# Decode attention over a long cache: V in runs of eight keys, p turned in column tiles, mask by matmul, another order at the end, and eight filler matmuls a pair

## The chip, the cores and the metric

One core of one Trainium2 chip. The metric is the device time of one execution in microseconds (us), the median of several. Single executions of one kernel lie within about 1% of each other in the first rounds (322.6 to 325.8 us for the kernel before), so differences of less than 1% are read only from several rounds against the kernel before on the same chip. A run that is more than 1.5% above the fastest of its kernel counts as slow; ratios use the other runs alone, unless said otherwise. A ratio is the mean time of one kernel's fast runs over that of the other's in the same rounds, so it is not quite the ratio of the medians quoted beside it.

TensorE is called PE below, its weight loads PEld, VectorE DVE, ScalarE ACT, GpSimd POOL. SPq is the wait of a queue's DMA issues for a free buffer.

## The reference, cut to what matters

```python
# x: 4 tokens x 448, bf16. k_cache, v_cache: [4, 8 heads, 8192, 256] bf16; the last 2,048 keys count
def _A_ref(x, k_cache, v_cache, wq, wo):          # two query heads share one key head
    q = (x @ wq)...
    k, v = k_cache[:, :, Sk - W:, :], v_cache[:, :, Sk - W:, :]
    p = softmax(einsum(q, k) * Dh ** -0.5)
    return einsum(p, v) @ wo
x = x + _A_ref(layernorm(x), ...);  x = x + ffn(layernorm(x))     # layer 1
x = x + _A_ref(layernorm(x), ...);  x = x + ffn(layernorm(x))     # layer 2, same cache, same weights
```

The work is 64 "pairs" of (token, layer, key head). Each pair reads 1 MB of K and 1 MB of V, of which some is still held from the first layer. In all some 105 MB go through the DMA queue in a little over 300 us.

## The kernel before

The kernel is written as a list of operations with ranks and assumed durations. At build time a small scheduler puts them into one fixed order for each engine; nothing is decided on the chip. For one pair, in the order of its chain (cut):

```python
# two loads of K (512 KB each) into free half buffers, each transposed in place by the DVE
g.dma(pos - KLEAD, 1 << 19, ... half[cell[0]] <- ksrc[:, 2048 * hf:2048 * hf + 2048])
g.op(DVE, 1.18, pos, tr, w=(kk[hf],))
# two loads of V: runs of four keys, 2,048 bytes each
vsrc = A_v_cache[t, kvh, s0:s0 + WIN, :].rearrange("(a q g) d -> q a g d", a=4, q=128)
g.dma(pos + VLAG, 1 << 19, ... half[cell[0]] <- vsrc[:, 2 * hv:2 * hv + 2, :, :], run=2048)

def scores(e):                                     # 32 matmuls of 128 columns, four column groups
    for ce in range(8):
        for hf in range(2):
            for x in range(2):
                e.matmul(Sb[s_][qd:qd + 8, 0:128], lhsT=qe[q_]..., rhs=kt[...])
# DVE: maximum of each row; PE: spread it over the partitions; DVE: maximum per head (two columns),
# then a masked sum that picks each partition's own head:
g.op(DVE, 0.2, pos, lambda e: e.scalar_tensor_tensor(out=nb[0:104, 2:4], in0=negm[s_][0:104, :], scalar=1.0,
     in1=nmask[0:104, :], op0=ALU.mult, op1=ALU.mult, accum_out=nb[0:104, 0:1]), ...)
# ACT: exp with that as bias, into praw
def turn(e):                                       # p to the layout that V asks for: 4 matmuls, 128 weights each
    for c in range(2):
        for h in range(2):
            e.matmul(Yb[p_][:, 64 + 32 * c:96 + 32 * c], lhsT=praw[s_][0:104, c0:c0 + 128], rhs=selt[h]...)
# ACT: copy to pT; PE: 16 matmuls with V (pv) of 256 columns; ACT, DVE, PE: the pair's output
```

On PE every matmul is two instructions, a weight load and the matmul itself (4,776 of each in the profile below).

Of the kernel before, what the change touches and what calls it, by code (L numbers as in the profile page):

```python
# [31 lines left out]
KLEAD = 2.2  # L32
VLAG = 1.3
# [12 lines left out]
MMV = 0.034  # L46
TAIL = {"pe": 0.2, "dve": 0.12, "act": 0.15, "pool": 0.1, "sp": 0.05}
# [232 lines left out]
def build(nc, A_x, A_k_cache, A_v_cache, A_wq, A_wo, B_x, B_w_gate, B_w_up, B_w_down, out):  # L280
# [3 lines left out]
    with ExitStack() as es:  # L284
# [12 lines left out]
        pmax = [tiny[:, 12 + s:13 + s] for s in range(NS)]  # L297
        tsel = sb("tsel", [128, 4, B], BF16)
        selt = [sb(f"selt{h}", [128, 2, 4, 2, 2], BF16) for h in range(2)]
        small = sb("small", [128, 11 + 6 * NS + 4 * NY + B + 4], FP32)  # L300
        rmask = small[:, 11 + 6 * NS + 4 * NY:11 + 6 * NS + 4 * NY + B]
        rvec = small[:, 11 + 6 * NS + 4 * NY + B:11 + 6 * NS + 4 * NY + B + 4]
        nmask = small[:, 9 + 2 * NS + 4 * NY:11 + 2 * NS + 4 * NY]
        nbias = small[:, 11 + 2 * NS + 4 * NY:11 + 6 * NS + 4 * NY]
# [21 lines left out]
        praw = [sb(f"praw{s}", [128, 258], BF16) for s in range(NS)]  # L326
        pT = [sb(f"pT{s}", [128, 2, 2, 4, 2, 2], BF16) for s in range(NY)]
# [48 lines left out]
        ivt = identb[:, :].rearrange("p (h x z n) -> p h x z n", h=2, x=2, n=2)  # L376
        for h in range(2):
            for y in range(2):
                for x in range(2):
                    g.op(DVE, 0.1, R0, lambda e, h=h, y=y, x=x: e.tensor_copy(selt[h][:, x, :, y, :], ivt[:, h, x, 0:4, :]),  # L380
                         r=("identb",), w=(f"selt{h}{y}{x}",))
        idq = identb[:, :].rearrange("p (q z n) -> p q z n", q=4, n=2)
        g.op(DVE, 0.2, R0, lambda e: e.tensor_reduce(
            nmask[:, :], idq[:, :, 0:4, :].rearrange("p q a n -> p n q a"), AX.XY, ALU.add), r=("identb",), w=("nmask",))
        for s_ in range(NS):
            g.op(DVE, 0.2, R0, lambda e, s_=s_: e.memset(Sb[s_][:, :], 0.0), w=(f"s{s_}",), bank=(f"S{s_}",))
            g.op(DVE, 0.2, R0, lambda e, s_=s_: e.memset(praw[s_][:, :], 0.0), w=(f"praw{s_}",))
# [44 lines left out]
        def norm(t, rank, x):  # L432
# [30 lines left out]
            gp(lambda e: e.tensor_tensor(s[:, 8:9], s[:, 5:6], expo[:, 0:1], op=ALU.pow), (k + "h", "expo"), (k + "r2",))  # L463
# [15 lines left out]
        def qproj(ts, rank):  # L479
# [5 lines left out]
            for b, (zb, z, bank) in enumerate(banks):  # L485
# [13 lines left out]
                for c0, c1, rr, kw in ((0, 3, XN, dict(w=(z,))), (3, 4, XE, dict(acc=(z,)))):  # L499
                    g.op(PE, 0.43 * (c1 - c0), rank, lambda e, zb=zb, b=b, c0=c0, c1=c1: q_mm(e, zb, b, c0, c1),  # L500
                         r=rr + tuple(f"wq{c}" for c in ((0, 1, 2) if c0 == 0 else (30, 31))), bank=(bank,), **kw)
# [34 lines left out]
        def ffn_row(ts, rank):  # L536
# [24 lines left out]
            for gi, (z, bank, w) in enumerate((("z", "Z", "wg"), ("z2", "Z2", "wu"))):  # L561
                g.op(PE, 1.28, rank, lambda e, gi=gi: gu(e, gi, 0, 3), r=XN + (w + "a",), w=(z,), bank=(bank,))
                g.op(PE, 0.5, rank, lambda e, gi=gi: gu(e, gi, 3, 4), r=XE + (w + "b0", w + "b1"), acc=(z,), bank=(bank,))
# [25 lines left out]
            g.op(PE, 1.5, rank, down, r=("wb", "wd"), acc=tuple(f"row{t}" for t in ts), bank=("A",))  # L589
# [119 lines left out]
        assert len(seq) == 2 * B * HKV and len(set(seq)) == len(seq)  # L709
        k_held, v_held = {}, {}  # L710
# [3 lines left out]
        def pair(pos, si, side, nside, t, layer, kvh):  # L714
# [3 lines left out]
            else:  # L718
                kc, kk = [[], []], [f"k{pos}_{hf}" for hf in range(2)]
                ksrc = A_k_cache[t, kvh, s0:s0 + WIN, :].rearrange("(p j) d -> p (j d)", p=128)  # L720
                for hf, cell in enumerate(kc):
                    g.dma(pos - KLEAD, 1 << 19, lambda e, cell=cell, hf=hf: e.dma_start(  # L722
# [8 lines left out]
            else:  # L731
                vsrc = A_v_cache[t, kvh, s0:s0 + WIN, :].rearrange("(a q g) d -> q a g d", a=4, q=128)
                vs = [[], []]
                for hv, cell in enumerate(vs):
                    g.dma(pos + VLAG, 1 << 19, lambda e, cell=cell, hv=hv: e.dma_start(  # L735
                        half[cell[0]][:, :].rearrange("p (a g d) -> p a g d", a=2, g=4),
                        vsrc[:, 2 * hv:2 * hv + 2, :, :]), None, w=(f"v{t}_{kvh}_{hv}",), run=2048, cell=cell)
# [3 lines left out]
            def scores(e):  # L741
                last = None
                for ce in range(8):
                    for hf in range(2):
                        kt = half[kc[hf][0]][:, :].rearrange("p (l g c r v) -> p c v g l r", l=2, g=4, c=4, v=2)
                        for x in range(2):
                            qd = 64 * hf + 32 * x
                            last = e.matmul(Sb[s_][qd:qd + 8, 0:128], lhsT=qe[q_][:, ce, :, :].rearrange("p a n -> p (a n)"),  # L748
                                            rhs=kt[:, ce // 2, ce % 2, 2 * x:2 * x + 2, :, :], start=(ce == 0),
# [6 lines left out]
            o = g.op(PE, 0.8, pos - SLEAD, scores, r=tuple(kk) + (f"qe{q_}",), w=(f"s{s_}",), bank=(f"S{s_}",))  # L756
            if not keep_k:
                o.rel = tuple(kc)
            g.op(DVE, 0.21, pos, lambda e: e.tensor_reduce(  # L759
                pmax[s_][0:104, :], Sb[s_][0:104, 0:128], AX.X, ALU.max),  # L760
                r=(f"s{s_}",), w=(f"pmax{s_}",), bank=(f"S{s_}",))
            g.op(PE, 0.1, pos, lambda e: e.matmul(  # L762
                Sb[s_][0:104, 128:160].rearrange("p (q x) -> p q x", q=4), lhsT=pmax[s_][0:104, 0:1].broadcast_to([104, 104]),
                rhs=identb[0:104, :].rearrange("p (q x) -> p q x", q=4)[:, :, 0:8], start=True, stop=True,
                skip_group_check=True), r=(f"pmax{s_}", "identb"), w=(f"m{s_}",), bank=(f"S{s_}",))
            g.op(DVE, 0.16, pos, lambda e: e.tensor_reduce(  # L766
                negm[s_][0:104, :], Sb[s_][0:104, 128:160].rearrange("p (k n) -> p n k", n=2), AX.X, ALU.max, negate=True),
                r=(f"m{s_}",), w=(f"negm{s_}",), bank=(f"S{s_}",))
            nb = nbias[:, 4 * s_:4 * s_ + 4]
            g.op(DVE, 0.2, pos, lambda e: e.scalar_tensor_tensor(  # L770
                out=nb[0:104, 2:4], in0=negm[s_][0:104, :], scalar=1.0, in1=nmask[0:104, :], op0=ALU.mult, op1=ALU.mult,
                accum_out=nb[0:104, 0:1]), r=(f"negm{s_}", "nmask"), w=(f"nb{s_}",))
            g.op(SCA, 0.38, pos, lambda e: e.activation(  # L773
                praw[s_][0:104, 2:258].rearrange("p (g r h l) -> p h g r l", g=2, h=2, l=2)[:, 0, :, :, :],
                Sb[s_][0:104, 0:128].rearrange("p (g l r) -> p g r l", g=2, l=2), ACT.Exp, bias=nb[0:104, 0:1]),
                r=(f"s{s_}", f"nb{s_}"), w=(f"praw{s_}",), bank=(f"S{s_}",))

            def turn(e):
                last = None
                for c in range(2):  # L780
                    for h in range(2):
                        c0 = 128 * c + 2 - 2 * h
                        last = e.matmul(Yb[p_][:, 64 + 32 * c:96 + 32 * c], lhsT=praw[s_][0:104, c0:c0 + 128],  # L783
                                        rhs=selt[h][0:104, :, :, :, :].rearrange("p x a y n -> p (x a y n)"),
                                        start=(c == 0 and h == 0), stop=False, skip_group_check=True)
                return last
            g.op(PE, 0.12, pos, turn,
                 r=(f"praw{s_}",) + tuple(f"selt{h}{y}{x}" for h in range(2) for y in range(2) for x in range(2)),
                 w=(f"yp{p_}",), bank=(f"Y{p_}",))
            g.op(SCA, 0.2, pos, lambda e: e.activation(  # L790
                pT[p_][:, :, :, :, :, :].rearrange("p c x a y n -> p (c x a y n)"), Yb[p_][:, 64:128], ACT.Copy),
# [3 lines left out]
                rhs=pT[p_][:, :, :, :, :, :].rearrange("p c x a y n -> p y (c x a) n")[:, 0, :, :], start=False,  # L795
# [6 lines left out]
            def pv(e, hv):  # L802
                last = None
                for a in range(2):
                    for gg in range(4):
                        last = e.matmul(Yb[p_][32 * gg:32 * gg + 4, 256:512],  # L806
                                        lhsT=pT[p_][:, gg % 2, gg // 2, 2 * hv + a, :, :].rearrange("p y n -> p (y n)"),
# [163 lines left out]
```

## Time and profile before

| | before |
|---|---|
| time, median (3 runs at first) | 324.81 us (323.2 to 325.83) |
| span in the profile | 320.3 us |
| bytes moved | 105.16 MB |
| V halves and K halves loaded | 88 and 88, of 512 KB |

The page's rows of clock and DMA, the stages and the chain in the last token are shown and read in the prediction. Four more lines of the same page matter later: the engines' busy times with their instruction counts, the packets, the queue that the page calls "instruction" (packets, MB, share of the 16 DMA engines' span), and the shares of the chain that ended last.

```profile
PE 222.0 (69%) x4776; PEld 136.6 (43%) x4776; DVE 212.4 (66%) x776; ACT 75.2 (23%) x222; POOL 89.2 (28%) x227
...
DMA packets 42369, 105.16 MB, mean 328 GB/s; under 512 B 3144, under 2 KB 7248, under 8 KB 41936
...
q8 instruction: 37, 0.61, 0.7%
...
DMA 40%; PE 23%; DVE 16%; SPq 15%; issue 3%; ACT 2%; POOL 0%; DVEq 0%
```

The reader is to see four things. The chain runs mostly over transfers (DMA 40%, and SPq 15% for loads that wait for a buffer). PE is busy for 69% and stands in the chain with 23%. "issue", time in which an engine waited for nothing that the profile shows, is 3%. And the instruction queue looks like nothing at all, 37 packets and 0.7%.

### The profile page before, as it was taken

To read this page: it belongs to the slowest core of one execution; us is meant where nothing else is said; L and a number is where in the kernel's file an instruction comes from. 1 tells how busy PE (TensorE), PEld (TensorE's weight loads), DVE (VectorE), ACT (ScalarE), POOL (GpSimd) and SP (SyncE) were. 2 spreads that over 40 slices of the span, in tenths; PEclk is the share of its full clock that TensorE was granted. 3 is DMA by queue.
4 is the path that set the end of the run, shared out by engine and by line. 5 is a ranking of instruction groups with operands and counts; after the bars stand their busy time and mean duration, and the time that the engine had idled before them with its cause. 6 is when DMAs were issued, how large, how long until landed. Compare 5 with 4: busy or idle time off the path is not lost.

```text
span 320.3 us, 11153 instructions
## 1 busy us (share of the span) xinstructions
PE 222.0 (69%) x4776; PEld 136.6 (43%) x4776; DVE 212.4 (66%) x776; ACT 75.2 (23%) x222; POOL 89.2 (28%) x227
## 2 busy tenths in 40 slices
PE   1746455546458768678669878796788788688965
PEld 0334232223124445344247555443455446356544
DVE  7396655564244769977656799877677983844642
ACT  0122111121012233212233233132323232023410
POOL 1712211113002333224214323342244322214420
PEclk9999999999999995658875655576958755555975
DMA  7999999999998999999959999999899999708000
GB/s 280 350 404 393 392 395 398 394 393 337 327 395 304 380 393 400 360 398 383 388 205 366 388 398 382 380 389 396 309 315 377 398 368 398 264 8 323 2 3 2
DMA packets 42369, 105.16 MB, mean 328 GB/s; under 512 B 3144, under 2 KB 7248, under 8 KB 41936
## 3 DMA queue, kind: packets, MB, share of 16 engines
q1 hardware_dynamic: 42320, 104.45, 87.9%
q8 instruction: 37, 0.61, 0.7%
q14 instruction: 12, 0.10, 0.1%
HBM read 104.44 MB, written 0.00 MB: 326 GB/s over the span
## 4 chain that ended last, share of the span: by engine, by line
DMA 40%; PE 23%; DVE 16%; SPq 15%; issue 3%; ACT 2%; POOL 0%; DVEq 0%
DMA half<-in_A_k_cache_dram 22%; DMA half<-in_A_v_cache_dram 13%; DVE half L727 9%; PE S L748 8%; SPq L735 6%; SPq L722 6%; PE Y L806 6%; DMA wg_sb<-in_B_w_gate_dram 5%; SPq L407 3%; DVE oh L820 2%; PE Z L558 2%; PE Z L496 1%; PE Z L612 1%; PE Y L826 1%; PE A L858 1%
## 5 line engine op out<-in xcount | busy, mean ns | idle before, releaser
L727 DVE STREAM_TRANSPOSE half<-half 128x1024 uint32<-128x1024 uint32 x88 | 108.8, 1238 | 19.4 <-DMA half<-in_A_k_cache_dram 19.1
L806 PE MATMUL Y<-half,pT 128*4 128x256 bf16 x1024 | 60.8, 356 | 21.0 <-DMA half<-in_A_v_cache_dram 17.9
L816 POOL TENSOR_TENSOR small<-small 128x2 f32<-128x2 f32 x64 | 44.3, 697 | 73.2 <-DVE small L798 66.0
L748 PE MATMUL S<-half,qe 128*8 128x128 bf16 x2048 | 58.9, 279 | 6.0 <-DVE half L727 2.3
L748 PEld LDWEIGHTS S<-half,qe 128*8 128x8 bf16 x2048 | 45.1, 108 | 12.7 <-DVE half L727 3.9
L752 POOL TENSOR_TENSOR qe<-qc,tiny 128x64 bf16<-128x64 bf16 x64 | 18.7, 293 | 93.9 <-PE S L748 71.0
L818 ACT ACTIVATE oh<-Y 128x256 bf16<-128x256 f32 x64 | 24.5, 384 | 77.4 <-PE Y L806 77.2
L806 PEld LDWEIGHTS Y<-half,pT 128*4 128x4 bf16 x1024 | 22.0, 94 | 34.7 <-DMA half<-in_A_v_cache_dram 21.8
L773 ACT ACTIVATE praw<-S,small 104x128 bf16<-104x128 f32 x64 | 22.9, 366 | 58.9 <-DVE small L770 58.7
L820 DVE SCALAR_TENSOR_TENSOR oh<-oh,small,Y 128x256 bf16<-128x256 bf16 x64 | 30.0, 471 | 9.0 <-ACT oh L818 8.2
L759 DVE TENSOR_REDUCE tiny<-S 104x1 bf16<-104x128 f32 x64 | 18.4, 287 | 23.4 <-PE S L748 23.1
L826 PE MATMUL Y<-tiny,oh 128*128 128x2 bf16 x128 | 12.9, 172 | 18.9 <-DVE oh L820 18.4
L790 ACT ACTIVATE pT<-Y 128x64 bf16<-128x64 f32 x64 | 14.1, 223 | 40.9 <-PE Y L783 38.3
L826 PEld LDWEIGHTS Y<-tiny,oh 128*128 128x128 bf16 x128 | 8.3, 107 | 28.1 <-DVE oh L820 24.8
L858 PE MATMUL A<-wo_sb,oT 128*4 128x448 bf16 x140 | 16.3, 454 | 4.3 <-DVE oT L831 4.1
L783 PE MATMUL Y<-selt,praw 104*128 104x32 bf16 x256 | 17.3, 187 | 1.3 <-ACT praw L773 1.3
L793 PE MATMUL Y<-pT,tiny 128*128 128x32 bf16 x64 | 12.5, 197 | 7.9 <-ACT pT L790 7.7
L783 PEld LDWEIGHTS Y<-selt,praw 104*128 104x128 bf16 x256 | 11.7, 104 | 12.5 <-issue 9.1
L766 DVE TENSOR_REDUCE small<-S 104x2 f32<-104x32 f32 x64 | 11.3, 183 | 6.3 <-PE S L762 6.1
L762 PE MATMUL S<-identb,tiny 104*104 104x32 bf16 x64 | 14.4, 240 | 1.6 <-DVE tiny L759 1.5
L459 POOL TENSOR_SCALAR st<-st 128x1 f32<-128x1 f32 x16 | 4.3, 267 | 38.7 <-DVE st L448 38.6
L442 PE MATMUL Z<-st,small 128*128 128x2 f32 x32 | 9.1, 355 | 8.1 <-DVE st L439 7.4
(120 smaller groups left out, 245.9 us busy)
## 6 DMA issues: line engine op xcount, KB each, us to landing
half<-in_A_k_cache_dram SPq DMA_DIRECT2D x88, 512.0 KB, 7.1
half<-in_A_v_cache_dram SPq DMA_DIRECT2D x88, 512.0 KB, 7.1
wo_sb<-in_A_wo_dram SPq DMA_DIRECT2D x8, 448.0 KB, 12.6
wq_sb<-in_A_wq_dram SPq DMA_DIRECT2D x3, 1024.0 KB, 6.8
wd_sb<-in_B_w_down_dram SPq DMA_DIRECT2D x1, 1568.0 KB, 18.3
wg_sb<-in_B_w_gate_dram SPq DMA_DIRECT2D x1, 1344.0 KB, 15.5
wu_sb<-in_B_w_up_dram SPq DMA_DIRECT2D x1, 1344.0 KB, 15.9
wq_sb<-in_A_wq_dram SPq DMA_DIRECT2D x2, 256.0 KB, 10.2
```

Source lines behind the costliest of these rows:

```text
L722: g.dma(pos - KLEAD, 1 << 19, lambda e, cell=cell, hf=hf: e.dma_start(half[cell[0]][:, :], ksrc[:, 2048 * hf:2048 * hf + 2048]), None, w=( ...
L727: return e.transpose(a, a)
L735: g.dma(pos + VLAG, 1 << 19, lambda e, cell=cell, hv=hv: e.dma_start(half[cell[0]][:, :].rearrange("p (a g d) -> p a g d", a=2, g=4), vsrc ...
L748: last = e.matmul(Sb[s_][qd:qd + 8, 0:128], lhsT=qe[q_][:, ce, :, :].rearrange("p a n -> p (a n)"), rhs=kt[:, ce // 2, ce % 2, 2 * x:2 * x ...
L773: g.op(SCA, 0.38, pos, lambda e: e.activation(praw[s_][0:104, 2:258].rearrange("p (g r h l) -> p h g r l", g=2, h=2, l=2)[:, 0, :, :, :], ...
L783: last = e.matmul(Yb[p_][:, 64 + 32 * c:96 + 32 * c], lhsT=praw[s_][0:104, c0:c0 + 128], rhs=selt[h][0:104, :, :, :, :].rearrange("p x a y ...
L806: last = e.matmul(Yb[p_][32 * gg:32 * gg + 4, 256:512], lhsT=pT[p_][:, gg % 2, gg // 2, 2 * hv + a, :, :].rearrange("p y n -> p (y n)"), r ...
L816: g.op(POOL, 0.25, pos, lambda e: e.tensor_tensor(ri[p_][:, :], rs[p_][:, :], expo[:, 1:3], op=ALU.pow), r=(f"rs{p_}", "expo"), w=(f"ri{p_ ...
L818: g.op(SCA, 0.28, pos, lambda e: e.activation(oh[pos % 2][:, :], Yb[p_][:, 256:512], ACT.Copy), r=(f"y{p_}",), w=(f"oh{pos % 2}",), bank=( ...
L820: g.op(DVE, 0.4, pos, lambda e: e.scalar_tensor_tensor(out=oh[pos % 2][:, :], in0=oh[pos % 2][:, :], scalar=lomask[:, 0:1], in1=Yb[p_][:, ...
L826: last = e.matmul(Yb[p_][:, 2 * dh:2 * dh + 2], lhsT=oh[pos % 2][:, :].rearrange("p (m e) -> p e m", e=2)[:, dh, :], rhs=osel[:, :], start ...
L858: last = e.matmul(Ab[32 * k:32 * k + B, 0:D], lhsT=oT[si % 2][:, k % 2, k // 2, :], rhs=wo_sb[:, 4 * kvh + k, :], start=False, stop=False, ...
```

## The change

The intent: V packets of 4,096 bytes instead of 2,048, so that the queue moves the same bytes sooner. That gives p another layout, so its turn is done in sixteen small column tiles instead of four wide ones. The masked sum leaves the DVE and becomes a second small matmul on PE. K of the last pairs is loaded later (tail order). Eight matmuls whose result nobody reads go in front of the scores of each pair, to keep PE's clock up. And the scheduler's assumed durations are set to measured ones. Cut to its core:

```diff
+KTAIL = 0.4
+FILL = 8
-    g.dma(pos - KLEAD, 1 << 19, ...                                     # K
+    g.dma(pos - KLEAD if pos <= LAST1 else pos + KTAIL, 1 << 19, ...
-    vsrc = A_v_cache[...].rearrange("(a q g) d -> q a g d", a=4, q=128)  # runs of 2,048 bytes
+    vsrc = A_v_cache[...].rearrange("(p j) d -> p (j d)", p=128)         # runs of 4,096 bytes
 def scores(e):
+    for i in range(FILL):
+        qd = 32 * (i % 4)
+        e.matmul(Sb[s_][qd:qd + 8, 160:512], lhsT=identb[:, 0:8],
+                 rhs=identb[:, 0:32].unsqueeze(1).broadcast_to([128, 11, 32]), start=True, stop=True, ...)
+def spread(e):                                  # a matmul more: adds "far" where the head isn't the partition's own
+    e.matmul(Sb[s_][0:104, 128:160], lhsT=identb[0:104, 0:104], rhs=far[0:104, :, :]..., start=True, stop=False)
-g.op(DVE, 0.2, pos, lambda e: e.scalar_tensor_tensor(... accum_out=nb[0:104, 0:1]) ...
 def turn(e):
-    for c in range(2):
-        for h in range(2):
-            e.matmul(Yb[p_][:, 64 + 32 * c:96 + 32 * c], lhsT=praw[s_][0:104, c0:c0 + 128], ...)
+    for gg in range(4):
+        for b in range(4):
+            e.matmul(Yb[p_][32 * b:32 * b + 32, 64 + 16 * gg:80 + 16 * gg],
+                     lhsT=praw[s_][0:104, 32 * gg:32 * gg + 32], rhs=selt[b]...)
-g.op(PE, 1.5, rank, down, ...                   # assumed durations, here and in a dozen more places
+g.op(PE, 0.8, rank, down, ...
```

## The prediction

> **What bounds the kernel now.** I read the page first, then the windows by stage, then the chain of waits, then the timeline of single pairs. A "pair" is one (token, layer, head): 64 in all, each with two K halves and two V halves of 512 KB; layer 1 finds 20 heads of both still held, so 88 halves of K and 88 of V are loaded. First the page: the DMA rows by slice, and the groups that the change touches.

> ```profile
> PEclk9999999999999995658875655576958755555975
> DMA  7999999999998999999959999999899999708000
> GB/s 280 350 404 393 392 395 398 394 393 337 327 395 304 380 393 400 360 398 383 388 205 366 388 398 382 380 389 396 309 315 377 398 368 398 264 8 323 2 3 2
> ...
> L748 PE MATMUL S<-half,qe 128*8 128x128 bf16 x2048 | 58.9, 279 | 6.0 <-DVE half L727 2.3
> ...
> L766 DVE TENSOR_REDUCE small<-S 104x2 f32<-104x32 f32 x64 | 11.3, 183 | 6.3 <-PE S L762 6.1
> ```

> The reader is to see a queue that is full up to the 34th slice (8 us each) and a tail of some 30 us with almost no traffic. So two bounds follow each other: the transfers, then a chain of compute. The windows view, by stage, says the same with numbers:

> ```profile
> 100.00:263.00 163.00, 124.76 (x2903) 78.55 (x2899) 128.15 (x442) 48.36 (x145) 51.44 (x125) 0.70 0.98 365
> 263.00:285.60 22.60, 17.50 (x361) 10.84 (x353) 13.23 (x53) 4.48 (x12) 5.74 (x16) 0.50 0.67 255
> 285.60:306.50 20.90, 18.76 (x482) 12.65 (x478) 10.82 (x63) 6.41 (x23) 9.19 (x21) 0.72 0.36 129
> 306.50:320.30 13.80, 7.64 (x213) 6.57 (x201) 4.21 (x22) 1.37 (x4) 1.68 (x6) 0.54 0.01 2
> ```

> (The columns are PE, weight loads, DVE, ACT, POOL, then granted clock, DMA share, GB/s.) From 100 to 263 us the queue ran at 365 GB/s where a full stretch (40 to 60 us, the same view) has 395: 163 x (1 - 365/395) = 12.4 us were lost there to loads that waited for a free buffer. From 263 us it is the last token's own path: its feed-forward and projection (22.6 us), its eight pairs of layer 1 (20.9 us, PE busy 90%) and the closing feed-forward (13.8 us).

> The chain of waits in the second of these stages shows what the DVE does there:

> ```profile
> 273.21 1.15 DVE half L727
> 274.37 0.05 DVE oT L831
> 274.42 1.14 DVE half L727
> ...
> 275.95 1.16 DVE half L727
> ...
> 277.56 1.15 DVE half L727
> 278.71 0.12 DVE xn L446
> 278.83 0.07 DVE st L448
> 278.90 1.43 PE Z L496 x7
> ```

> Transposes of K that is needed only at the very end stand in front of the normalisation that the last token's q waits for.

> And PE's clock, from the timeline, the 32 score matmuls of a pair at 104.9 us and at 262.1 us:

> ```profile
> 104.86 0.62 PE L748 MATMUL S<-half,qe 128*8 128x128 bf16 x32
> ...
> 262.10 1.02 PE L748 MATMUL S<-half,qe 128*8 128x128 bf16 x32
> ```

> The same work takes 0.62 us at full clock and 1.02 us at half. Before 100 us the clock row shows 1.0, yet 32 score matmuls took 1.07 us there (windows of that line): PE was cold, the profile only had no clock event yet.

> [...] clock stretches are multiples of 3.41 us, at 1.0 or 0.5. [...] I counted for every such window the columns streamed, with four matmuls on the four column groups as one. Of the cold windows from 96 us on, all ten with 3,168 or more were followed by full clock, none with 3,108 or fewer; warm windows stayed warm at 2,756 and more, with one exception (2,952). [...] Trace: scores start in groups of four, and (1.02 - 0.62) x 1000 / 8 = 50 ns per group is just what 128 columns differ by. [...] In this trace's packet records 2,048-byte packets have a median of 84 ns and 4,096-byte ones 159 ns, so two of the small cost 9 ns more.

> **The change, part by part.**

> V in runs of eight keys. V packets double from 2,048 to 4,096 bytes, 22,528 of them become 11,264. By mean durations, 22,528 x 89.3 ns / 16 engines = 125.7 us becomes 11,264 x 169.2 / 16 = 119.1 us: 6.6 us. 76 of 88 V halves are issued before 263 us or so, where the queue is the bound: 5.7 us, and I take 5.0, as it isn't always full.

> p turned in column tiles. Four matmuls with 128 weights become sixteen with 32, on four column groups. The four take 0.29 us (timeline). The nearest thing here is the select of the q projection, sixteen matmuls with 32 weights each: 0.30 us. So no cost. exp writes its 128 columns in a plain order; I take its 366 ns as unchanged.

> Mask by matmul. The DVE loses the masked sum and its accumulator read (152 and 82 ns, overlapped to 0.17 us in the timeline): 64 x 0.17 = 10.9 us of DVE's 212, off a chain every pair goes through. The reduce keeps its 32 inputs, so its 183 ns. A second matmul joins the spread: two of them took 0.33 us, one 0.25, so 0.08 us more. Net -0.09 us on the pair's latency; over the eight last pairs 0.7 us.

> Fillers. Eight of 352 columns on four groups are 704 columns in time: 0.29 us at full clock, 0.59 at half, per pair. They come after the waits of the scores, so they fill no idle time; they lengthen the path from a transposed K to its scores. In return they feed the clock: from 99 to 308 us the mean window has 2,568 columns, 22 of 61 windows warm. With 51 pairs there, 704 x 51 / 61 = 589 more make 3,157, about the threshold; I estimate 65% warm instead of 36%. Cost per pair 0.65 x 0.29 + 0.35 x 0.59 = 0.40 us; gain 0.29 x (0.40 on scores + 0.58 on PV + 0.15 on the output projection) = 0.33 us. In the DMA-bound part this is a wash. In the last eight pairs it is not: they run cold from 285.7 to about 297 us, and dense work with fillers (1,024 + 1,024 + 704 + some 400 to 600 columns a pair) passes the threshold within two windows. I take 1.5 us net.

> Tail order. K of the last 11 pairs ranks behind the V of the pair before, not three pairs ahead. Before, six K halves took the free buffers from 263.6 us on, and their transposes stood on the chain above; with K and V in turn about two of the six come after it: 2 x 1.2 = 2.4 us.

> Stalls. The schedule is fixed at build time from assumed durations, and those of PE and POOL become truer if PE is warm; the DVE, over 90% busy from 120 to 140 us, is relieved. I give this a quarter of the 12.4 us: 3.1 us.

> Sum: 5.0 + 0.7 + 1.5 + 2.4 + 3.1 = 12.7 us off 324.8: about 312.

> **The rivals.** (1) The clock doesn't catch. The fillers then cost 0.59 us on pairs with PE already at 15 to 17 of 20 us busy: 51 x 0.59 = 30 us more PE work, perhaps a third of it visible, 10 us. Against it: the score matmuls, of the same shape and columns of weights, evidently count in the windows above. Time then about 322. (2) The clock catches nearly everywhere after 100 us. Then pairs save up to 1.1 us on PE for 0.29, most stalls go, and only the queue and the tail remain: about 303. For it: the mean lies on the threshold, and a faster kernel makes windows denser. Against it: windows with projections or waits have 1,000 to 2,000 columns. (3) V is hidden anyway: the queue's gain turns into waits for free buffers, since a buffer comes free only when PE is done with it. Then the 5 us shrink to 2, time about 315. The 12.4 us of stalls speak for it, the DMA share of 0.98 in that stage against. (4) The new fixed order falls unluckily, with a stall of its own at a token's change like the 4 us around 165 us (slice 21): 317 or so.

> **Range and chances.** Centre 312, between rivals 2 and 3. The five terms are independent enough, each good to a half, and the order of the schedule adds some 4 us either way: 304 to 320 for 8 in 10. Two per cent faster is below 318.3: 0.84. Within two per cent: 0.13. Slower than 331.3 asks for rival 1 and a bad order: 0.03.

> **What would show each step.** V: 4,096-byte packets alone, some 31,100 packets instead of 42,369, full stretches at 400 to 405 GB/s, DMA's share of 16 engines' span times span down 6 us. Mask: no accumulator read in the pairs, DVE busy down about 11 us. Turn: 1,024 records with a busy time near 17 to 20 us. Clock: half-clock stretches after 100 us down to a third of the time; scores with fillers 0.9 us when warm, 1.6 cold. Tail: alternating K and V issues after 250 us, fewer transposes ahead of the last norm, and the stretch from 263 us to the end 52 us instead of 57. I am wrong if the queue is still stalled by 12 us or more, if the clock stays at half for most of the middle, or if the tail is no shorter.

The time of a column, which the fillers' estimate needs, can be read in the trace of the kernel before: where the matmuls with V (L806, 256 columns) follow each other in groups of four, the groups start 109 ns apart at full clock and 213 ns at half (medians). By that, 128 columns differ by 52 ns, and 704 columns are 0.30 us and 0.59 us.

## The result, and the profile after

The changed kernel took 338.1 us (median of 4, 335.38 to 340.1), the kernel before 324.0 in the same rounds (4 runs). The ratio is 1.0426, with a 95% interval of 1.0316 to 1.0536, all runs fast: it is slower, by some 13.8 us. The prediction was wrong in direction. The result is correct.

The changed kernel's page, the same rows as of before, and the groups that the change touched:

```profile
PE 243.9 (72%) x6120; PEld 154.5 (46%) x6120; DVE 207.6 (61%) x651; ACT 75.8 (22%) x222; POOL 89.4 (26%) x227
...
PEclk9975555555569957759976959696755965599785
DMA  7999999999989996998999959999889877876000
GB/s 277 350 405 401 403 403 403 403 383 322 405 313 329 374 352 231 323 406 311 409 372 382 373 188 334 356 358 378 280 286 372 241 269 247 263 286 266 6 3 2
DMA packets 31115, 105.33 MB, mean 312 GB/s; under 512 B 3144, under 2 KB 7248, under 8 KB 30672
...
q8 instruction: 48, 0.79, 0.9%
...
PE 42%; DMA 18%; DVE 15%; SPq 14%; issue 7%; ACT 2%
PE Y L820 9%; PE S L762 9%; DMA half<-in_A_v_cache_dram 9%; DVE half L736 9%; PE S L753 7%; SPq L731 5%; DMA wd_sb<-in_B_w_down_dram 5%; SPq L415 5%; DMA half<-in_A_k_cache_dram 4%; SPq L744 4%; PE Z L566 2%; PE Z L620 2%; PE A L873 2%; DVE oh L835 2%; PE Z L504 2%
...
L762 PEld LDWEIGHTS S<-half,qe 128*8 128x8 bf16 x2048 | 47.5, 106 | 24.9 <-issue 19.1
L753 PE MATMUL S<-identb 128*8 128x352 bf16 x512 | 41.0, 402 | 18.4 <-DVE half L736 7.1
...
L796 PE MATMUL Y<-selt,praw 104*32 104x16 bf16 x1024 | 18.6, 177 | 2.5 <-issue 2.4
```

Much is as predicted: 31,115 packets, 401 to 405 GB/s where the queue is full, 18.6 us of records for the turn. But from the twelfth slice on the GB/s row is mostly below before's, so the queue is filled less than before, not faster. The chain has moved from transfers (40% to 18%) to PE (23% to 42%), the fillers (L753) alone stand in it with 7%, and "issue" rose from 3% to 7%, from 9.6 to 23.7 us of the span. The score's weight loads (L762) were idle 19.1 us on "issue". In the kernel before, the same group (L748) had:

```profile
L748 PEld LDWEIGHTS S<-half,qe 128*8 128x8 bf16 x2048 | 45.1, 108 | 12.7 <-DVE half L727 3.9
```

By stage, the windows of the changed kernel, cut where the chain's stages lie in it (columns as in the prediction):

```profile
100.00:263.00 163.00, 128.79 (x3432) 82.11 (x3425) 112.49 (x326) 42.55 (x129) 48.08 (x117) 0.76 0.92 335
263.00:298.70 35.70, 27.72 (x705) 18.47 (x704) 21.39 (x71) 8.71 (x25) 8.93 (x22) 0.67 0.77 262
298.70:324.50 25.80, 20.05 (x671) 13.89 (x667) 14.53 (x56) 7.55 (x25) 9.57 (x22) 0.93 0.39 146
324.50:338.00 13.50, 7.54 (x205) 6.52 (x205) 4.35 (x23) 1.17 (x4) 1.66 (x5) 0.58 0.01 3
```

From 100 to 263 us the queue had 335 GB/s instead of 365, although PE's clock was higher (0.76 instead of 0.70). The loss is spread. The casts of q into its layout, one for each token's change to the second layer, mark the stages:

| us | 1st token's second q | 2nd | 3rd | 4th | end of span |
|---|---|---|---|---|---|
| before | 103.0 | 165.1 | 230.1 | 284.8 | 320.3 |
| changed | 100.6 | 166.1 | 238.4 | 298.7 | 338.0 |
| lost in the stage | | 3.4 | 7.3 | 5.6 | 3.8 |

What is "issue"? The list of PE's weight-load waits names it (in all, times, longest, in us). First the changed kernel, then before:

```profile
PEld S L762 <- issue: 19.1, 54, 3.7
PEld Y L820 <- DMA half<-in_A_v_cache_dram: 12.6, 15, 1.4
...
PEld S L777 <- issue: 6.3, 12, 3.0
...
PEld Y L796 <- issue: 4.9, 12, 1.9
```

```profile
PEld Y L783 <- issue: 9.1, 30, 0.4
...
PEld Z L450 <- issue: 3.4, 6, 0.9
...
PEld S L762 <- issue: 2.4, 8, 0.4
```

The totals differ by a factor of two, but the last column tells more: in the kernel before, waits on nothing are short, 0.4 us in the pairs; in the changed one they last up to 3.7 us. One of them, in the changed kernel's timeline of PE:

```profile
126.22 0.47 PE L753 MATMUL S<-identb 128*8 128x352 bf16 x8 [0.21 <-DVE half L736]
126.52 0.22 PE L762 MATMUL S<-half,qe 128*8 128x128 bf16 x2
128.93 1.02 PE L762 MATMUL S<-half,qe 128*8 128x128 bf16 x30 [2.19 <-issue]
```

PE did the fillers and two of the 32 score matmuls of a pair. Then it stood for over two microseconds in the middle of a loop whose inputs were all there, and did the other thirty. Nothing in the program can explain a stop at that place.

```
PE passed the boundary before | packet of 16 KB started, landed | PE stopped, resumed
121.93                        | 126.51, 127.44                  | 126.5, 128.93
182.98                        | 186.86, 187.82                  | 187.4, 189.16
305.2                         | 309.41, 310.33                  | 308.1, 311.76
```

Each time the packet starts 3.9 to 4.6 us after the boundary before, takes 0.9 to 1.0 us, and PE goes on 1.3 to 1.5 us after it has landed. The theory which the experiments had to try: PE runs out of instructions, and waits where it needs the next 256 sooner than that.

### The profile page after: what moved, and what is told of

The parts are those of the page before. It is cut to its first block, busy times and chain, and to the rows that moved or that the text cites.

```text
span 338.0 us, 13720 instructions
## 1 busy us (share of the span) xinstructions
PE 243.9 (72%) x6120; PEld 154.5 (46%) x6120; DVE 207.6 (61%) x651; ACT 75.8 (22%) x222; POOL 89.4 (26%) x227
## 2 busy tenths in 40 slices
DMA packets 31115, 105.33 MB, mean 312 GB/s; under 512 B 3144, under 2 KB 7248, under 8 KB 30672
## 4 chain that ended last, share of the span: by engine, by line
PE 42%; DMA 18%; DVE 15%; SPq 14%; issue 7%; ACT 2%
PE Y L820 9%; PE S L762 9%; DMA half<-in_A_v_cache_dram 9%; DVE half L736 9%; PE S L753 7%; SPq L731 5%; DMA wd_sb<-in_B_w_down_dram 5%; SPq L415 5%; DMA half<-in_A_k_cache_dram 4%; SPq L744 4%; PE Z L566 2%; PE Z L620 2%; PE A L873 2%; DVE oh L835 2%; PE Z L504 2%
## 5 line engine op out<-in xcount | busy, mean ns | idle before, releaser
L820 PE MATMUL Y<-half,pT 128*4 128x256 bf16 x1024 | 57.8, 338 | 12.7 <-DMA half<-in_A_v_cache_dram 9.9
L831 POOL TENSOR_TENSOR small<-small 128x2 f32<-128x2 f32 x64 | 44.3, 694 | 82.1 <-DVE small L812 80.9
L762 PE MATMUL S<-half,qe 128*8 128x128 bf16 x2048 | 57.0, 265 | 7.9 <-issue 7.8
L762 PEld LDWEIGHTS S<-half,qe 128*8 128x8 bf16 x2048 | 47.5, 106 | 24.9 <-issue 19.1
L753 PE MATMUL S<-identb 128*8 128x352 bf16 x512 | 41.0, 402 | 18.4 <-DVE half L736 7.1
L766 POOL TENSOR_TENSOR qe<-qc,tiny 128x64 bf16<-128x64 bf16 x64 | 18.6, 292 | 101.5 <-PE S L762 87.5
L785 DVE TENSOR_REDUCE small<-S 104x1 f32<-104x32 f32 x64 | 11.6, 185 | 16.6 <-PE S L779 13.8
L796 PE MATMUL Y<-selt,praw 104*32 104x16 bf16 x1024 | 18.6, 177 | 2.5 <-issue 2.4
L753 PEld LDWEIGHTS S<-identb 128*8 128x8 bf16 x512 | 9.5, 90 | 23.7 <-DVE half L736 10.2
L796 PEld LDWEIGHTS Y<-selt,praw 104*32 104x32 bf16 x1024 | 15.9, 103 | 7.3 <-issue 4.9
L812 DVE TENSOR_REDUCE small<-Y 128x2 f32<-128x32 f32 x64 | 11.7, 184 | 10.8 <-PE Y L807 10.3
L846 DVE TENSOR_TENSOR oT<-Y,small 128x4 bf16<-128x4 f32 x64 | 10.1, 159 | 13.0 <-PE Y L841 12.0
L777 PE MATMUL S<-far,identb 104*104 104x32 bf16 x64 | 14.7, 236 | 4.5 <-issue 2.9
```

The costliest lines, as they stand in the source:

```text
L753: e.matmul(Sb[s_][qd:qd + 8, 160:512], lhsT=identb[:, 0:8], rhs=identb[:, 0:32].unsqueeze(1).broadcast_to([128, 11, 32]), start=True, stop ...
L762: last = e.matmul(Sb[s_][qd:qd + 8, 0:128], lhsT=qe[q_][:, ce, :, :].rearrange("p a n -> p (a n)"), rhs=kt[:, ce // 2, ce % 2, x, :, :], s ...
L766: g.op(POOL, 0.25, pos - SLEAD - 1, lambda e: e.tensor_tensor(qe[q_][:, :, :, :], qc[t][:, kvh, :, :].unsqueeze(2).broadcast_to([128, 8, 4 ...
L796: last = e.matmul(Yb[p_][32 * b:32 * b + 32, 64 + 16 * gg:80 + 16 * gg], lhsT=praw[s_][0:104, 32 * gg:32 * gg + 32], rhs=selt[b][0:104, :, ...
L820: last = e.matmul(Yb[p_][32 * gg:32 * gg + 4, 256:512], lhsT=pT[p_][:, gg, 2 * hv + x, :, :].rearrange("p y n -> p (y n)"), rhs=half[vs[hv ...
L831: g.op(POOL, 0.69, pos, lambda e: e.tensor_tensor(ri[p_][:, :], rs[p_][:, :], expo[:, 1:3], op=ALU.pow), r=(f"rs{p_}", "expo"), w=(f"ri{p_ ...
```

## The experiments

The theories in dispute:

- **Instructions (supply).** 256 PE instructions can't, as a rule, pass in less than some 5.5 to 6.5 us while the queue is full of data (an estimate from the packets' records: 3 to 4 us until the packet starts, 1.0 for the packet, 1.4 until PE goes on). With the projections and feed-forwards spread over them, a pair of the kernel before has 9,626 / 64 = 150 PE instructions, one of the changed kernel 12,321 / 64 = 193: 24 more from the turn (12 matmuls, two instructions each), 16 from the fillers, 2 from the spread. From 100 to 263 us before does 43 pairs, 3.8 us each: 256 instructions pass in 3.8 x 256 / 150 = 6.5 us, just about what the supply allows, and would have to pass in 5.0 us at 193.
- **Time (latency).** The fillers stand on the path from a transposed K to its scores, 0.30 us when PE is warm and 0.55 when it is cold, measured from the first filler to the first score.
- **Order.** The new durations or the tail order give a fixed order that falls badly.
- **V.** The larger packets, or the turn that they need, cost by themselves.

Runs against the kernel before on the same chip (323.56 us, 7 runs):

**e1: no fillers** (the changed kernel):

```diff
-FILL = 8
+FILL = 0
```

> The changed kernel without its fillers; every engine's order of the other work is as in the changed kernel. Theory T (the fillers' own PE time of 0.30 to 0.55 us ahead of a pair's scores, in 64 pairs, is the loss): about 15 us faster than changed, 320 to 325. Theory I (PE runs dry of instructions: the changed trace has gaps of 0.6 to 3.7 us inside runs of matmuls, put down to issue, some 16 us in sum, and none over 0.5 us before; 16 of the 42 more PE instructions of a pair are the fillers'): also faster, the issue gaps fewer but not all gone. Theory O (the new fixed order and the tail order are the loss): still 335 or more. PE colder in every case.

Measured 326.63 us (324.81 to 328.77), ratio 1.0077 (1.0004 to 1.0151). So the fillers are worth 1.0426 - 1.0077 = 3.5%, 11.3 us. The rest of the change, for which 11 us of gain had been predicted, is no gain at all. PE still stops: 13 times, 15.4 us, at the same two places modulo 256. One of them stands between two groups of the matmuls with V, in this kernel's timeline:

```profile
169.81 0.50 PE L820 MATMUL Y<-half,pT 128*4 128x256 bf16 x12
172.89 0.81 PE L820 MATMUL Y<-half,pT 128*4 128x256 bf16 x12 [2.58 <-issue]
```

**e2: fillers with no work in them** (the changed kernel, as many fillers of 2 columns instead of 352):

```diff
-    e.matmul(Sb[s_][qd:qd + 8, 160:512], lhsT=identb[:, 0:8],
-             rhs=identb[:, 0:32].unsqueeze(1).broadcast_to([128, 11, 32]), start=True, stop=True, ...)
+    e.matmul(Sb[s_][qd:qd + 8, 160:162], lhsT=identb[:, 0:8], rhs=identb[:, 0:2], start=True, stop=True, ...)
```

> Eight fillers of 2 columns instead of 352: the same number of PE instructions as the changed kernel, hardly any streaming time. Theory T: like the run without fillers, within 3 us. Theory I: stays close to the changed kernel, over 330, with issue gaps as before. If PE's warmth matters, this is also the cold kernel with all the instructions.

Measured 336.87 us (335.69 to 338.33), ratio 1.0379 (1.0311 to 1.0446). They now take 0.054 us in front of the scores, 64 x 0.054 = 3.5 us if every bit were seen, and still cost 1.0379 - 1.0077 = 3.0%, 9.8 us. So most of what the fillers cost doesn't come from their columns. PE stops 12 times in this run's profile, 15.7 us. That sum isn't larger than without fillers, and so the sum of clear stops is not a measure of the time lost; I come back to this.

**e3: the same columns in few instructions** (the changed kernel, two fillers over the whole array, 704 columns in time as before, 4 instructions instead of 16):

```diff
-    for i in range(FILL):
-        qd = 32 * (i % 4)
-        e.matmul(Sb[s_][qd:qd + 8, 160:512], lhsT=identb[:, 0:8], ...
+    for i in range(2):
+        e.matmul(Sb[s_][:, 160:512], lhsT=identb[:, :], ...
```

> Two fillers of 352 columns on the full array instead of eight on four column groups: the same 704 columns of time and clock activity, 4 instructions instead of 16. Theory T: as slow as the changed kernel, 335 to 340. Theory I: clearly faster than it, 325 or less, with fewer issue gaps, and PE as warm as in the changed kernel.

Measured 337.33 us over all four runs (333.7 to 340.78, two of them slow), ratio of the fast ones 1.0313 (1.0227 to 1.0399). PE stops less, 4 times and 8.7 us (its profile is of a slow run), but these fillers take 0.40 us warm and 0.70 us cold in front of the scores, more than the packed ones. So time in front of the scores costs too: 1.0313 - 1.0077 = 2.4%, 7.6 us, for some 35 us of it in all (33 pairs cold, 30 warm). Neither the supply theory nor the time theory holds alone.

**e4: without the tail order** (the changed kernel):

```diff
-    g.dma(pos - KLEAD if pos <= LAST1 else pos + KTAIL, 1 << 19, ...
+    g.dma(pos - KLEAD, 1 << 19, ...
```

> The changed kernel with the K loads of the last eleven pairs ranked as before (three pairs ahead). Theory O in the tail: the stretch after the third token's projection (238 us) gets shorter by 5 us or more, 330 or less. Theories T and I: within 3 us of the changed kernel; by the prediction's own step it would be 2.4 us slower.

Measured 342.88 us over all four runs (341.33 to 347.13, the highest one slow), ratio of the fast ones 1.056 (1.0487 to 1.0633). So the tail order isn't the cause; it seems to help in the changed kernel, by about 1.3%, but the two intervals overlap.

Before: 324.22 us. The same theories from the other side, by parts added to the kernel before.

**e5: only instructions** (the kernel before, with 13 matmuls of 2 columns in front of the scores, which brings it to the instruction count of the changed kernel without fillers):

```diff
+    for i in range(13):
+        qd = 32 * (i % 4)
+        e.matmul(Sb[s_][qd:qd + 8, 160:162], lhsT=identb[:, 0:8], rhs=identb[:, 0:2], start=True, stop=True, ...)
```

> The kernel before, with 13 fillers of 2 columns in front of a pair's scores: 26 more PE instructions a pair, so as many in all (some 11,300) as the changed kernel without fillers has, with the old turn, old V, old order. The eight tiny fillers took 0.054 us a pair, so 13 take about 0.09: 64 x 0.09 = 5.6 us of PE if all of it shows, 1 to 3 us by what is usually hidden. Theory I: 330 or more, and gaps over 0.5 us inside runs of matmuls, ten or so, where the kernel before has none. Theory T: 327 or less, no such gaps.

Measured 336.62 us (333.49 to 337.89), ratio 1.0365 (1.0302 to 1.0427). This is the cleanest run: V, the turn, the mask, the order and the durations are those of before, the columns are nothing, and 11.8 us are lost. In front of the scores the thirteen take 0.083 us, 64 x 0.083 = 5.3 us at most. PE, which had no stop before, has seven, 10.0 us in all, at 193 or 194 modulo 256. One of them, in its timeline, and the line of its weight-load waits:

```profile
125.89 0.92 PE L753 MATMUL S<-half,qe 128*8 128x128 bf16 x25
129.52 0.29 PE L753 MATMUL S<-half,qe 128*8 128x128 bf16 x7 [2.71 <-issue]
```

```profile
PEld S L753 <- issue: 5.3, 5, 3.0
```

Again the 32 scores of one pair are cut in two, 25 and 7.

**e6: only the tail order** (the kernel before, the diff of e4 the other way round, with `LAST1` and `KTAIL`):

> The kernel before with the tail order alone (K of the last eleven pairs ranked after the V of the pair ahead). By the prediction's step 2.4 us faster, about 321; by what undoing it cost the changed kernel (about 1.3%), up to 4 us. Theory O (the tail order starves the tail of loads) says slower.

Measured 325.33 us over all six runs (321.06 to 327.16, three of them slow), ratio of the fast ones 0.9924 (0.9855 to 0.9994): 2.5 us faster, by an interval that nearly reaches 1. It rests on leaving out three of six runs: the mean of all six, 324.8 us, is that of all runs of before, 324.6. In its profile (a run of 324.2 us) three transposes of K come after the last token's q, where before has none, as the prediction had it; but from the third token's q to the end it takes 89.6 us and before 90.2, so the 2.4 us are not seen there.

**e7: only the mask by matmul** (the kernel before, with the changed kernel's spread, its reduce to one column and no masked sum):

```diff
+    e.matmul(Sb[s_][0:104, 128:160]..., lhsT=identb[0:104, 0:104],
+             rhs=far[0:104, :].unsqueeze(1).broadcast_to([104, 16, 2]), start=True, stop=False, ...)
-g.op(DVE, 0.2, pos, lambda e: e.scalar_tensor_tensor(... accum_out=nb[0:104, 0:1]) ...
```

> The kernel before with the mask by matmul alone (the mask's row is broadcast from two columns, for room). By the prediction's step 0.7 us faster from the last pairs and a little more where the DVE was full: 321 to 324. DVE busy down by about 11 us. Theory I: 128 PE instructions more in all, too few to matter.

Measured 323.25 us over all six runs (319.87 to 325.99, one slow), ratio of the fast ones 0.9937 (0.9882 to 0.9993): about 2 us.

**e8: the changed kernel without fillers, with the assumed durations of before:**

```diff
-FILL = 8
+FILL = 0
-g.op(PE, 0.8, rank, down, ...       # and the other durations likewise
+g.op(PE, 1.5, rank, down, ...
```

> The changed kernel without fillers, scheduled with the durations assumed in the kernel before. Theory O (the new assumed durations order the work badly): 3 us or more faster than the run without fillers (326.6). Theory I (it is the 26 more PE instructions a pair of turn and mask that keep the gain of V away): within 2 us of it, with the same kind of gaps.

Measured 331.0 us over all four runs (328.25 to 334.52, one slow), ratio of the fast ones 1.0178 (1.0111 to 1.0245). So the new durations seem to help here, by about 1% (the intervals just overlap); it isn't they that spoil the order.

Before: 325.17 us. The good parts together, and V with few instructions.

**e9: tail order and mask** (the edits of e6 and e7, both on the kernel before):

> The kernel before with tail order and mask by matmul, nothing else. If the two gains (ratios 0.992 and 0.994) add up: 0.986, about 319 to 320. Theory I: hardly any stalls at every 256th PE instruction, 3 us in sum or less.

Measured 323.55 us, ratio 0.9968 (0.992 to 1.0017). The two gains don't add up; this is no more than 1 us and may be nothing.

**e10: tail order, mask and twelve matmuls of 2 columns** (e9 with the edit of e5, twelve instead of thirteen), as many PE instructions (11,293) as in the changed kernel without fillers (11,297, and 11,287 with the old durations), but V and the turn of before:

> The same with twelve 2-column fillers a pair, so that it has as many PE instructions as the changed kernel without fillers (some 11,300), but V in runs of four, the old turn and the old assumed durations. Theory I: 10 us or more slower than the run without them, 329 to 333, with 10 us or more of stalls at every 256th instruction; and slower than the changed kernel without fillers (326.6) by what V in runs of eight is worth at equal instruction count, about 5 us.

Measured 335.7 us over all four runs, ratio of the two fast ones 1.038 (1.0302 to 1.0459): 4.1% above the run before it, 13.4 us, again for instructions with hardly any columns. PE stops 11 times, 18.6 us. Against e8, which has the same instruction count and V in runs of eight, it is 2.0% slower; so V's larger packets may be worth something, between 1 and 6 us by my estimate, since the twelve also take up to 64 x 0.08 = 5 us of their own in front of the scores.

**e11: tail order, mask and the new durations**, the changed kernel's three parts that add almost no instructions:

```diff
+KTAIL = 0.4
-g.op(PE, 1.5, rank, down, ...       # and the other durations likewise
+g.op(PE, 0.8, rank, down, ...
-g.op(DVE, 0.2, pos, lambda e: e.scalar_tensor_tensor(... accum_out=nb[0:104, 0:1]) ...
+    e.matmul(Sb[s_][0:104, 128:160]..., lhsT=identb[0:104, 0:104], rhs=far..., start=True, stop=False, ...)
```

> Tail order and mask by matmul, scheduled with the durations that the change assumes. The changed kernel without fillers lost about 1% with the old durations; if they help here as well, 315 to 318; if that was chance of the order, 318 to 323.

Measured 322.3 us (320.1 to 324.46, six runs, all fast), ratio 0.9929 (0.987 to 0.9988). By the median of all runs this is the best version found, 0.7% faster than before by its ratio, with 9,758 PE instructions.

**e12: V in runs of eight with a turn of four matmuls** (the changed kernel without fillers). ACT writes exp four times, with biases that blot out three of four row groups each time, so that the turn needs only four matmuls:

```diff
+    for b in range(4):                            # ACT: 4 exps instead of 1
+        e.activation(praw...[:, b, :, :], Sb[s_]..., ACT.Exp, bias=nb[0:104, b:b + 1])
 def turn(e):
     for gg in range(4):
-        for b in range(4):
-            e.matmul(Yb[p_][32 * b:32 * b + 32, ...], lhsT=praw[s_][0:104, 32 * gg:32 * gg + 32], ...)
+        e.matmul(Yb[p_][:, 64 + 16 * gg:80 + 16 * gg], lhsT=praw[s_][0:104, 128 * gg:128 * gg + 128], ...)
```

> V in runs of eight with few PE instructions: the changed kernel without fillers, but exp writes p four times, each time with all but one block of rows masked to zero by its bias, so that the turn needs four matmuls instead of sixteen (24 PE instructions a pair less). Cost: three more ACT exps of 0.37 us in each pair's chain and a small DVE op. Theory I: the stalls at every 256th instruction vanish (3 us in sum or less), and the 5 us of V come out in the DMA-bound part, less up to 1.1 us a pair in the last eight pairs: 316 to 324, faster than the changed kernel without fillers (326.6). If V's gain is eaten by waits for free buffers instead (rival 3 of the prediction), it stays at 325 or more without stalls.

Measured 348.54 us over all six runs, ratio of the fast ones 1.0704 (1.0639 to 1.0769): the slowest of all. The lines of its page that tell why (its profile is of a slow run):

```profile
q8 instruction: 38, 0.62, 0.7%
...
L799 ACT ACTIVATE praw<-S,pen 104x128 bf16<-104x128 f32 x256 | 72.8, 372 | 46.2 <-DVE pen L794 46.1
```

The expectation failed. There is not one stop of PE's in it, with 38 instruction packets: the supply no longer limits, though the slower pace helps (256 instructions take 7.9 us here, the median). But each pair's chain has three exps more, 3 x 0.37 = 1.1 us, and a small DVE operation for their biases (and praw, four times as large, is one buffer where there were two, since no more fitted). Against e11, which has the same other parts and the V of before, that cost 1.0704 - 0.9929 = 7.8%, 25 us. The prediction had taken it that from 100 to 263 us the queue alone sets the pace, and that time added to a pair is seen only in the last eight. At 1.1 us that would have been 9 us. So a pair's own chain lies close behind the queue: about a third of 64 x 1.1 = 70 us was seen. How much of that the single buffer did, this run can't tell.

Before: 325.26 us. Two things that were still open.

**e13: tail order and durations without the mask** (e11 without its last two edits):

> The kernel before with the tail order and the change's assumed durations, no PE instruction added (9,626 as before). If the two PE instructions a pair of the mask gave back part of its gain through stalls, this is as fast as tail order plus mask plus durations (322) or faster: 318 to 322, with stalls at every 256th instruction below 2 us in sum.

Measured 326.17 us over all six runs (two slow), ratio of the fast ones 0.999 (0.9906 to 1.0075), so no gain and not what was expected; of e11's three parts the mask seems to be needed. Differences of this size are at the limit of what the runs can tell.

**e14: a quarter of V** (the changed kernel without fillers; each V load brings 512 of its 2,048 columns, and the buffers are zeroed at the start, since the rest is read too; the result is wrong, though it still passed the comparison, which is therefore a weak test of V):

```diff
-    half[cell[0]][:, :], vsrc[:, 2048 * hv:2048 * hv + 2048])
+    half[cell[0]][:, 0:512], vsrc[:, 2048 * hv:2048 * hv + 512])
+g.op(DVE, 14.0, R0 - 1, c_half, w=("hinit",))      # zero the buffers; all K and V loads wait for it
```

> Wrong results on purpose: the changed kernel without fillers (11,297 PE instructions), but each V load brings a quarter of its half (the rest of the buffer is zeroed once at the start, which costs some 15 us there), so 34 MB less go through the DMA queue. If the refill of PE's instructions is slow because its packets stand behind the data in a full DMA, the time from passing one 256th instruction to the start of the refill's packet falls from the median of 3.3 us towards 2 us or less, and the stalls shrink to a third or less although PE works more densely. If the refill's time is its own, it stays at 3 us or more and the stalls grow, to 20 us or more.

One run, 334.16 us, its state unknown. The zeroing delays the first q from 20.4 us (in e1) to 48.3, so I compare from the first q to the end of the span: 303 us in e1, 284 here. (The comparison is rough: at the first q, 11 halves of K and V had landed here and 4 in e1.) Its page, the packets and the chain:

```profile
DMA packets 31111, 70.66 MB, mean 213 GB/s; under 512 B 3144, under 2 KB 18512, under 8 KB 30672
...
q8 instruction: 44, 0.72, 0.9%
...
PE 49%; DVE 38%; issue 7%; ACT 4%; DMA 1%; POOL 0%; DVEq 0%; ACTq 0%
```

34.6 MB less went through the queue, which at 405 GB/s is 85 us of it, and the kernel became 19 us shorter: on the average over these 85 us, a microsecond taken off the queue was worth a quarter of one. It is an estimate from one run, and the first few microseconds may be worth more than the average, since the queue drops out of the chain on the way. DMA is down to 1% of the chain, so 284 us is about what the compute side of this kernel needs by itself. And the supply theory is seen at its root: the median time from a boundary to the start of its instruction packet, packets and boundaries taken in order, fell from 3.1 us (e1) to 1.2 us. So in these two runs the instruction packets wait longer with more data in the queue. The changed kernel's own trace agrees: after 324.5 us, where the DMA share is 0.01, its last two packets start 0.3 us before and 0.7 us after the boundary. PE still stopped five times (7.7 us), half of e1's 15.4 and not the third that was expected.

All runs of the ladder in one table (stops as defined above, in each run's profile):

| kernel | PE instructions | stops, us | ratio to before (95%) |
|---|---|---|---|
| before | 9,626 | 0 | 1 |
| tail, mask, durations (e11) | 9,758 | 3, 4.0 | 0.9929 (0.987 to 0.9988) |
| and V and the turn (e1) | 11,297 | 13, 15.4 | 1.0077 (1.0004 to 1.0151) |
| and eight fillers of 2 columns (e2) | 12,321 | 12, 15.7 | 1.0379 (1.0311 to 1.0446) |
| with 352 columns: the changed kernel | 12,321 | 9, 13.6 | 1.0426 (1.0316 to 1.0536) |
| before and 13 matmuls of 2 columns (e5) | 11,290 | 7, 10.0 | 1.0365 (1.0302 to 1.0427) |
| V in runs of eight, four exps (e12) | 9,749 | 0 | 1.0704 (1.0639 to 1.0769) |

In microseconds of 324 the ladder is -2.3, +4.8, +9.8, +1.5, together 13.8. Why the third step costs 9.8 us while the clear stops stay at 15 us is not fully explained. The count is too narrow: with stops at the same boundaries that fall together with a wait of PE's own taken in as well, it is 1.2 us in before, 19.6 in e1 and 27.3 in e2, 7.7 us between the last two; with the 3.5 us that the small fillers take by themselves, that is the right size. But such a stop may have been a wait anyway, so this is a plausible account and not a proof.

## Why the prediction was wrong, point by point

**The turn ("p turned in column tiles … So no cost") is the first step that failed.** The busy time was right, 18.6 us against 17.3. But twelve matmuls more are 24 PE instructions more in each pair, 1,536 in all, and the prediction gave an instruction no price of its own. Also its analogue was off for half the pairs: from the first weight load to the last matmul the turn took 0.29 us before and 0.37 in the changed kernel (median of 61 pairs; 0.27 at the tenth percentile, 0.62 at the ninetieth). How much of the loss is the turn's alone was not isolated from V: the two together are +4.8 us (e1 against e11), while 26 and 24 instructions a pair without the turn cost 11.8 and 13.4 us in e5 and e10.

**The fillers ("In the DMA-bound part this is a wash"; "I take 1.5 us net") are the second.** For their columns the balance was right: from the first filler to the first score it took 0.30 us warm and 0.55 cold, where 0.29 and 0.59 were predicted; 352 columns instead of 2 made 1.5 us, with overlapping intervals, and the clock paid for them: 36 of 67 windows of 3.4 us were at full clock between 98 and 327 us, against 18 of 67 with 2 columns (e2). That is 54% where 65% was predicted and 36% was before. (The mean clocks of two whole runs can't be compared: before 99 us the row of the kernel before stood at 1.0 although PE was cold, with 32 score matmuls in 1.07 us.) The prediction's limit, between 3,108 and 3,168 columns in a window, held only roughly in the changed kernel: windows went warm at 3,048 and 2,852, and two at 3,072 and 3,076 did not. A pair's fillers and scores took 0.94 us warm and 1.61 cold, as foreseen. What was missing is the sixteen instructions, 1,024 in all: with 2 columns they cost 9.8 us. The gain of 1.5 us became a loss of 11.3. The sign that named this rival (1), a clock that doesn't catch, did not appear; the loss had a reason that no rival held.

**V ("I take 5.0") failed too, in its sum.** In full stretches the packets were as predicted: 164.1 ns for 4,096 bytes from 40 to 60 us, where two of 2,048 had taken 2 x 87.8. But from 100 to 263 us the mean packet of 4,096 bytes rose from 169.2 ns to 177.5 (median 159 in both), and over the whole run all K and V packets took 249.0 us of the 16 engines against 246.2 before (246.2 in e1 as well). The predicted 6 us off "DMA's share times span" are not there. Rival (3), "V is hidden anyway", spoke of the right mechanism and was too mild. The queue waits for buffers that PE frees late. Its longest waits, by the queue's own list, before and then changed:

```profile
SPq L722 <- PE Y L806: 30.9, 17, 4.2
SPq L735 <- PE Y L806: 28.0, 11, 4.3
```

```profile
SPq L731 <- PE Y L820: 42.6, 17, 5.8
SPq L744 <- PE Y L820: 36.9, 15, 4.7
```

The wait of K's and V's loads for the matmuls with V rose from 58.9 to 79.5 us. By the average rate of the thin-V run, a quarter, even the predicted 6.6 us of queue would be worth about 1.6 us (a rough estimate from e14; the first microseconds may be worth more). What V brings alone, without any more instructions, was not isolated: the attempt (e12) put its cost on ACT instead.

**Mask, tail order and stalls ("0.7", "2.4", "3.1": 6.2 in all) came to 2.3 us together (e11).** The tail order did what was predicted to the order of the transposes, but its 2.4 us are not shown: 2.5 us alone (e6) only by leaving out three of six runs, 1.3% in the changed kernel with overlapping intervals (e4), nothing with the new durations (e13). By the prediction's own sign the tail was no shorter: from the third token's q to the end it takes 99.6 us in the changed kernel and 90.2 before. The mask alone gave 2 us, more than the predicted 0.7; of DVE's predicted 11 us busy only 212.4 - 207.6 = 4.8 went (4.6 in e7), presumably since the removed records overlapped others. The two together gave only 1 us (e9). The quarter of the stalls that was to be won back wasn't: instead of 12.4 us, 163 x (1 - 335/403) = 27.5 us of the middle stage were lost to an unfilled queue in the changed kernel.

Term by term: V and the turn -5.0 predicted, +4.8 measured; fillers -1.5 and +11.3; the other three -6.2 and -2.3. The differences are 9.8, 12.8 and 3.9 us, together the 26.5 us between -12.7 and +13.8.

**The premise behind all of it** was "a queue that is full up to the 34th slice", taken as the bound there. The queue was full, but PE and the chain of a pair were only a little behind. With the two limits that close together here, a lengthening of the second was seen (11.8 us in e5, 25 us in e12), and a relief of the first mostly was not (19 of 85 us in e14).

So what is shown: small matmuls with hardly any columns cost this kernel 3 to 4%, 9.8 to 13.4 us (e2 against e1, e5 and e10 against kernels without them). Their own time, 3.5 to 5.3 us in front of the scores, is too short for that, the more so as 35 us of such time cost only 7.6 us in e3. PE's stops without a cause in the program lie at every 256th instruction alone (193 or 194 modulo 256). In the changed kernel's nine the packet of instructions started 2.1 to 4.6 us after the boundary one block before, and PE went on 1.3 to 1.6 us after it had landed. And these packets come later when the data queue is full: 3.1 us after a boundary with V in full (e1), 1.2 us with a quarter of V (e14), by the medians. What is argued: that stops which coincide with other waits make up the rest of the loss. What is open: V's worth by itself, the turn's share, why the mean 4,096-byte packet became longer, whether the tail order helps, and how far below 9,626 instructions a further cut would still help.

## What to carry to other kernels

Give every PE instruction a price, not only its columns: count weight loads and matmuls in blocks (of 256 here, by the places of the stops), and compare the time in which PE would pass a block with the time in which the next one arrives while the queue is full (here some 5.5 to 6.5 us, the estimate above). Before you add fillers, try them with 2 columns: what they cost then is the price of their number (9.8 us for eight a pair in e2). And where a queue and a chain of compute are nearly in step, measure what a microsecond of each is worth by thinning one of them, before you credit a saving on either.
